# A square root moved one place forward in ScalarE's queue, and one PSUM evacuation split by K tile, at the start of a TensorE-bound kernel

## The chip, the cores and the metric

The kernel runs on one core of one Trainium2 chip. The metric is device microseconds of one launch. Engines are called as in the profile: PE is the matmul engine (PEld its weight loads), ACT is ScalarE, DVE is VectorE, POOL is GpSimd. All runs used here were of the fast state, with a mean granted PE clock of 0.999 or 1.0; where the text below calls a run slow, it means a longer run within that state. A run with several rounds was timed beside the kernel before on the same chip.

## The reference, cut to what matters

```python
xn = layernorm(x)                      # x: 2048 tokens x 512, bf16
y  = x + S5(xn) + SwiGLU(xn)           # S5: complex diagonal scan over the tokens
# SwiGLU: (silu(xn @ w_gate) * (xn @ w_up)) @ w_down, hidden size 1376
```

Only the start matters here: before the first gate matmul can run, tokens must be loaded, normalised and transposed. The kernel works in 4 chunks of 512 tokens. Chunk 0 is handled in 4 tiles of 128 tokens, each in halves of 256 columns (two K tiles of 128).

## The kernel before: the parts that matter

Every operation is added to a graph. A list scheduler orders ACT, DVE and POOL from estimated durations (`est`) and from order constraints (`od`, `order=`); PE keeps the order in which its tasks are added. Each engine then runs its list strictly in order. Statistics of chunk 0 (cuts marked with `# ...`):

```python
def ln_stat0(a, order):
    # DVE: bn_aggr -> mv[a] ...
    hold["sd%d" % a] = g.add("act", ... func=AF.Sqrt ...)      # the square root, on ACT
# DVE's order: r reciprocal, n normalise a half, b statistics of a half, s aggregate + square root
last = ln_stat0(0, (bn_full(0),))
for op, a, h in (("r", 0, 0), ("n", 0, 0), ("b", 1, 0), ("b", 1, 1), ("s", 1, 0), ("n", 0, 1), ("b", 2, 0),
                 ("r", 1, 0), ("n", 1, 0), ("n", 1, 1), ("b", 2, 1), ("s", 2, 0), ("b", 3, 0),
                 ("r", 2, 0), ("n", 2, 0), ("n", 2, 1), ("b", 3, 1), ("s", 3, 0), # ...
```

Transposes, evacuations and gate matmuls. One PSUM bank holds the transposes of every half tile:

```python
def xt_tile_fine(a, h):
    # PE: two 128x128 transposes of xn half h of tile a into PSUM bank `slot`
    # tiles 0 to 2: ACT copies 128x256 from PSUM to xnT ("xTev", hold["ev<a><h>"]); tile 3: DVE does
# ...
for q in range(4):                                   # token tile q
    for k0, k1 in ((0, 2), (2, 3), (3, 4)) if q == 0 else ((0, 2), (2, 4)):
        for n, (i, bk) in enumerate(tiles):          # 7 column blocks of the gate
            if k0 == 0 and n == (2 if q == 0 else 1): xt_tile_fine(q, 1)
            if k0 == 2 and n == 1 and q < 3:          xt_tile_fine(q + 1, 0)
            # PE: gate matmuls of K tiles k0 to k1-1, 128 columns each
seq = ["sd0", "ev00", "sd1", "ev01", "ev10", "ev11", "sd2", "ev20", "sd3", "ev21"]   # ACT's order
for a_, b_ in zip(seq, seq[1:]):
    hold[b_].od.add(hold[a_])
```

So tile 2's square root `sd2` stands behind `ev11`, the evacuation of tile 1's second half.

Of the kernel before, what the change touches and what calls it, by code (L numbers as in the profile page):

```python
# [14 lines left out]
AF = mybir.ActivationFunctionType  # L15
# [234 lines left out]
def bass_parallel_sum__ssm_conv_s5__swiglu_ffn__prompt_kernel(  # L250
# [30 lines left out]
    g = _Graph()  # L281
    es = ExitStack()
    with es:
        block = es.enter_context(nc.Block(no_gpsimd_drain=True))

        def sb(name, shape, dt):
            return es.enter_context(nc.sbuf_tensor(name, shape, dt))
# [11 lines left out]
        wg = sb("wg", [128, KT, FT * 128], B16)  # L299
# [30 lines left out]
        sd0 = sb("sd0", [128, 4], F32)  # L330
# [38 lines left out]
        def next_pair():  # L369
            for _ in range(NB // 2):  # L370
                b = 2 * (pair_ctr[0] % (NB // 2))
                pair_ctr[0] += 1
                if not (b in reserved or _bank_live(b) or _bank_live(b + 1)):
                    return b
            raise AssertionError("all PSUM pairs live")
# [4 lines left out]
        def BK(b):  # L380
            return [("bk", b, 0), ("bk", b, 1)]
# [60 lines left out]
        def loads_stage_b2():  # L442
# [13 lines left out]
              reads=[("ones",)], writes=[("ident",)], name="ident", est=300)  # L456
        g.add("pool", lambda e: e.iota(iot[:], pattern=[[1, TP]], base=0, channel_multiplier=0, allow_small_or_imprecise_dtypes=True),
              writes=[("iot",)], name="iota", est=1000)
# [3 lines left out]
        def act_table(func, order):  # L462
            g.add("act", lambda e: e.activation(out=sm[:, NSM - 1, 0:1], in_=epst[:], func=func, bias=epst[:, 0:1]), reads=[("epst",)], writes=[("sm", "_warm")],
                  name="act_warm", est=1500, order=order)
# [3 lines left out]
        def pe_warm(n, w=512, bk=None):  # L468
            if bk is None:
                bk = next_pair()  # L470

            def mm(e, bk=bk):
                for _ in range(n):
                    inst = e.matmul(pbank[:, bk, 0:w], lhsT=one.to_broadcast([128, 128]), rhs=one.to_broadcast([128, w]), start=True, stop=True)  # L474
                return inst
            g.add("pe", mm, writes=BK(bk), name="pe_warm", est=n * w * 0.84, ninst=n)
# [29 lines left out]
        hold = {}  # L506
# [18 lines left out]
        def ln_chunk0():  # L525
            def bn_full(a, order=()):
                return g.add("dve", lambda e: e.bn_stats(out=st0[:, a, 0, :], in_=x_sb[:, a, :]), reads=[("x", a)], writes=[("st0", a, 0)], name="bnst%d" % a, est=640, order=order)
            def recip(a, order):
                return g.add("dve", lambda e: e.reciprocal(out=rstd[:, a:a + 1], in_=sd0[:, a:a + 1]), reads=[("sd0", a)], writes=[("rstd", a)],  # L529
                             name="rstd%d" % a, est=140, order=order)  # L530
# [3 lines that stand above are left out]
                             ("r", 2, 0), ("n", 2, 0), ("n", 2, 1), ("b", 3, 1), ("s", 3, 0),  # L534
                             ("r", 3, 0), ("n", 3, 0), ("n", 3, 1)):
                if op == "r":
                    last = recip(a, (last,))
                elif op == "n":
                    last = ln_half(a, h, (last,))
                elif op == "b":  # L540
                    last = bn_half(a, h, (last,))
                else:
                    last = ln_stat0(a, (last,))
            hold["xn3"] = last
# [15 lines left out]
        def xt_tile_fine(a, h):  # L560
            slot = xt_pair[0]
            par = a == 3 and h == 1

            def tr2(e):
                if par:
                    e.transpose(out=ptr[:, slot, 512:524], in_=prow[:], identity=ident[0:12, 0:12])  # L566
                for j in range(2):
                    kt = h * 2 + j
                    inst = e.transpose(out=ptr[:, slot, j * 128:(j + 1) * 128],  # L569
                                       in_=xn_sb[:, a % NXN, kt * 128:(kt + 1) * 128], identity=ident[:])  # L570
                return inst
            g.add("pe", tr2, reads=[("xh", a, h), ("ident",)] + [("prow", k) for k in range(3) if par], writes=BK(slot), name="xT%d_%d" % (a, h), est=2 * 64 + 100 * par, ninst=2 + par)
            dst, src = xnT[:, 0, a % 4, 2 * h:2 * h + 2, :], ptr[:, slot, 0:256].rearrange("p (k t) -> p k t", k=2)
            wr = [("xnTh", a, h)] + ([("xnT", 0, a % 4)] if h else [])
            if a == 3:
                t = g.add("dve", lambda e: e.tensor_copy(out=dst, in_=src), reads=BK(slot), writes=wr, name="xTev%d_%d" % (a, h), est=320, order=(hold["xn3"],))
                if par:
                    g.add("dve", lambda e: e.tensor_copy(out=praw[:].rearrange("p k a -> p (k a)"), in_=ptr[:, slot, 512:524]),
                          reads=BK(slot), writes=[("praw", k) for k in range(3)], name="parTev", est=80, order=(t,))
            else:  # L580
                t = g.add("act", lambda e: e.activation(out=dst, in_=src, func=AF.Identity), reads=BK(slot), writes=wr, name="xTev%d_%d" % (a, h), est=340)  # L581
            hold["ev%d%d" % (a, h)] = t
# [154 lines left out]
        def ffn_mm(c, i, which, bk):  # L737
            fs = fsz[i]
            w = wg if which == "g" else wu

            def mm(e, bk=bk, w=w, i=i, fs=fs, c=c):
                for kt in range(KT):
                    inst = e.matmul(pbank[0:fs, bk, :].rearrange("p (j t) -> p j t", j=4), lhsT=w[:, kt, i * 128:i * 128 + fs], rhs=xnT[:, c % 2, :, kt, :],  # L743
                                    start=(kt == 0), stop=(kt == KT - 1))
                return inst
            g.add("pe", mm, reads=wres("wg" if which == "g" else "wu", i) + [("xnT", c % 2, j) for j in range(4)],
                  writes=BK(bk), name="mm_%s%d_%d" % (which, c, i), est=4 * 216, ninst=4)
# [17 lines left out]
        def ffn_gate_quarters(pairs):  # L765
            banks = {ip: next_pair() for ip in pairs}
            reserved.update(banks.values())
            tiles = [(2 * ip + k, banks[ip] + k) for ip in pairs for k in range(2)]
            xt_pair[0] = tiles.pop()[1]
            wbank = tiles[-1][1]  # L770
            pe_warm(9, 512, wbank)
            pe_warm(2, 128, wbank)
            ln_chunk0()
            xt_tile_fine(0, 0)
            pe_warm(2, 256, wbank)
            for q in range(4):
                for k0, k1 in ((0, 2), (2, 3), (3, 4)) if q == 0 else ((0, 2), (2, 4)):
                    for n, (i, bk) in enumerate(tiles):
                        if k0 == 0 and n == (2 if q == 0 else 1):
                            xt_tile_fine(q, 1)  # L780
                        if k0 == 2 and n == 1 and q < 3:
                            xt_tile_fine(q + 1, 0)
                        def mm(e, bk=bk, i=i, q=q, k0=k0, k1=k1):
                            for kt in range(k0, k1):
                                inst = e.matmul(pbank[:, bk, q * 128:(q + 1) * 128], lhsT=wg[:, kt, i * 128:(i + 1) * 128], rhs=xnT[:, 0, q, kt, :],  # L785
                                                start=(kt == 0), stop=(kt == KT - 1))
                            return inst
                        g.add("pe", mm, reads=[("wg", "a%d" % max(k - 1, 0)) for k in range(k0, k1)] + [("xnTh", q, k0 // 2)], writes=BK(bk), name="mm_gq%d_%d_%d" % (i, q, k0),
                              est=(k1 - k0) * 56, ninst=k1 - k0)
            reserved.clear()  # L790
            seq = ["sd0", "ev00", "sd1", "ev01", "ev10", "ev11", "sd2", "ev20", "sd3", "ev21"]
            for a_, b_ in zip(seq, seq[1:]):
                hold[b_].od.add(hold[a_])
            act_table(AF.Silu, (hold["ev21"],))
            hold["evac"] = g.tasks[-1]
            ffn_mm(0, NQ, "g", xt_pair[0])
            for ip in pairs:
                silu_pair(0, ip, banks[ip])
# [273 lines left out]
```

## Time and profile before

| | before |
|---|---|
| time, median of 3 runs | 180.33 us (180.17 to 180.47) |
| span of the profiled run | 178.5 us |
| PE between 30 and 170 us | busy 140.0 of 140.0 us |
| PE weight loads idle before tile 2's transposes | 0.63 us |

First the busy line and the chain line of the profile page of the kernel before.

```profile
PE 174.5 (98%) x936; PEld 83.8 (47%) x936; DVE 163.1 (91%) x285; ACT 87.5 (49%) x110; POOL 11.3 (6%) x21
...
PE 97%; ACT 1%; DVE 0%; issue 0%
```

Then a row of the table by windows (window and length in us, busy us and instruction count of PE, PEld, DVE, ACT, POOL, then clock and DMA):

```profile
30.00:170.00 140.00, 140.00 (x678) 64.10 (x676) 137.69 (x195) 65.35 (x76) 6.32 (x4) 1.00 0.15 40
```

From tile 2's transposes at 9.45 us to its last matmul, which ends at 176.15 us, PE never pauses in this trace. A microsecond saved on another engine in that stretch is worth nothing; one that lets PE start its long run sooner should be worth a microsecond. ACT between 7 and 9 us, in the timeline of the kernel before (start, duration, what; in brackets the idle time before it and who ended it; L581 is an evacuation, L521 a square root):

```profile
7.29 0.38 ACT L581 ACTIVATE xnT<-pb 128x256 bf16<-128x256 bf16 x1 [0.43 <-PE pb L569]
8.24 0.38 ACT L581 ACTIVATE xnT<-pb 128x256 bf16<-128x256 bf16 x1 [0.57 <-PE pb L569]
8.52 0.29 ACT L521 ACTIVATE sd<-mv,epst 128x1 f32<-128x1 f32 x1
```

DVE around that root, same view (L519 is the aggregate of tile 2's statistics, L529 the reciprocal of the root; tile 2 is normalised from 9.04 us on):

```profile
7.50 0.21 DVE L519 BATCH_NORM_AGGREGATE mv<-st 128x2 f32<-128x12 f32 x1
...
8.84 0.17 DVE L529 RECIPROCAL rstd<-sd 128x1 f32<-128x1 f32 x1 [0.84 <-ACT sd L521]
```

and PE's weight loads, same view (L569 are transposes, L785 gate matmuls, L743 the first full-width matmuls):

```profile
5.86 0.24 PEld L785 LDWEIGHTS pb<-xnT,wg 128*128 128x128 bf16 x4 [0.60 <-issue]
6.15 0.11 PEld L569 LDWEIGHTS pb<-ident,xn_sb 128*128 128x128 bf16 x2
...
7.99 0.82 PEld L785 LDWEIGHTS pb<-xnT,wg 128*128 128x128 bf16 x14
9.44 0.12 PEld L569 LDWEIGHTS pb<-ident,xn_sb 128*128 128x128 bf16 x2 [0.63 <-DVE xn_sb L514]
...
13.86 0.15 PEld L743 LDWEIGHTS pb<-xnT,wg 128*128 128x128 bf16 x2
```

The reader is to see the idle 0.57 us in front of ACT's evacuation at 8.24, the square root behind it, and 0.63 us in which PE waits for what depends on that root. Evacuation and root were queued in the wrong order: the root's input was ready at 7.71 us (end of DVE's aggregate), while ACT stood idle.

### The profile page before, as it was taken

Reading aid. Unit: us, or ns where it says so; the run is one execution under the profiler, and the core shown is the slowest. Engines: PE = TensorE matmul, PEld = TensorE weight load, DVE = VectorE, ACT = ScalarE, POOL = GpSimd, SP = SyncE. Lnnn points to the kernel's source line nnn. Section 1 sums busy time; section 2 is a strip of 40 time slices with the busy share of each in tenths; the row PEclk is TensorE's granted clock in tenths of the full one; section 3 lists DMA queues with packets and bytes.
Section 4 is the critical chain, followed back from the end, with each engine's and each line's share of the span. In section 5 each row is a group of like instructions: output and inputs, shape, how many; then the busy total and the mean of one; then the engine's idle time right before and its main releaser. Section 6 shows DMA issues by size and latency. Waiting matters only on the chain.

```text
span 178.5 us, 2422 instructions
## 1 busy us (share of the span) xinstructions
PE 174.5 (98%) x936; PEld 83.8 (47%) x936; DVE 163.1 (91%) x285; ACT 87.5 (49%) x110; POOL 11.3 (6%) x21
## 2 busy tenths in 40 slices
PE   8989999999999999999999999999999999999994
PEld 2785444444444444444444444444444444444743
DVE  2768988997999999999999999999899999999933
ACT  4459999799999765024565651000965620000000
POOL 3014200130000000260000000000000000000000
PEclk9999999999999999999999999999999999999999
DMA  5995563569450000001510000001000000001022
GB/s 169 376 326 118 119 121 119 128 133 333 131 94 0 0 0 0 0 29 62 123 26 0 0 0 4 0 29 59 29 0 4 0 0 0 0 0 49 14 88 88
DMA packets 22978, 12.37 MB, mean 69 GB/s; under 512 B 15192, under 2 KB 22968, under 8 KB 22968
## 3 DMA queue, kind: packets, MB, share of 16 engines
q1 hardware_dynamic: 22472, 11.54, 23.6%
q10 hardware_dynamic: 496, 0.69, 1.1%
q8 instruction: 7, 0.11, 0.3%
q14 instruction: 3, 0.02, 0.0%
HBM read 6.46 MB, written 2.10 MB: 48 GB/s over the span
## 4 chain that ended last, share of the span: by engine, by line
PE 97%; ACT 1%; DVE 0%; issue 0%
PE pb L743 35%; PE pb L940 21%; PE pb L953 16%; PE pb L857 15%; PE pb L785 3%; PE pb L474 2%; PE pb L820 2%; PE pb L830 1%; PE pb L569 1%; ACT xnT L581 0%; DVE xn_sb L514 0%; DVE x_sb L958 0%; ACT sd L521 0%; DVE rstd L529 0%; PE pb L566 0%
## 5 line engine op out<-in xcount | busy, mean ns | idle before, releaser
L897 DVE TENSOR_TENSOR_SCAN rot<-sm,car,rot 128x512 bf16<-128x512 f32 x32 | 39.0, 1267 | 0.1
L940 PE MATMUL pb<-wd,hT 128*128 128x512 bf16 (+3 forms) x198 | 38.8, 356 | 0.0
L743 PE MATMUL pb<-xnT,wu 128*128 128x512 bf16 x160 | 37.3, 379 | 0.0
L743 PE MATMUL pb<-xnT,wg 128*128 128x512 bf16 x132 | 31.3, 380 | 0.0
L953 PE MATMUL pb<-W,hss 128*128 128x512 bf16 (+2 forms) x144 | 28.3, 356 | 0.0
L857 PE MATMUL pb<-xnT,BT 128*128 128x512 bf16 x128 | 28.1, 379 | 0.0
L940 PEld LDWEIGHTS pb<-wd,hT 128*128 128x128 bf16 (+1 forms) x198 | 18.5, 97 | 19.9
L755 ACT ACTIVATE sg<-pb 128x1024 bf16<-128x1024 f32 x20 | 20.1, 1024 | 9.2 <-PE pb L743 8.1
L743 PEld LDWEIGHTS pb<-xnT,wu 128*128 128x128 bf16 x160 | 15.6, 98 | 18.9 <-issue 0.2
L810 ACT ACTIVATE uf<-pb 128x1024 bf16<-128x1024 f32 x20 | 20.5, 1027 | 7.2 <-PE pb L743 6.1
L953 PEld LDWEIGHTS pb<-W,hss 128*128 128x128 bf16 x144 | 13.4, 98 | 14.3
L743 PEld LDWEIGHTS pb<-xnT,wg 128*128 128x128 bf16 x132 | 12.7, 98 | 15.7 <-issue 0.4
L857 PEld LDWEIGHTS pb<-xnT,BT 128*128 128x128 bf16 x128 | 12.5, 98 | 15.1
L864 ACT ACTIVATE u_sb<-pb 128x1024 bf16<-128x1024 f32 x16 | 16.2, 1021 | 5.9 <-PE pb L857 5.5
L958 DVE TENSOR_TENSOR x_sb<-pb,x_sb 128x512 bf16<-128x512 f32 (+2 forms) x18 | 11.1, 623 | 3.5 <-PE pb L953 3.5
L812 DVE TENSOR_TENSOR hT<-sg,uf 128x1024 bf16<-128x1024 bf16 x20 | 13.5, 684 | 0.6 <-ACT uf L810 0.5
L503 ACT ACTIVATE xn_sb<-x_sb,nmr,rstd 128x512 bf16<-128x512 bf16 x8 | 6.0, 803 | 9.7 <-DVE nmr L500 9.7
L839 ACT ACTIVATE sg<-pb 96x1024 bf16<-96x1024 f32 x2 | 2.0, 1020 | 17.1 <-PE pb L820 17.1
L888 DVE TENSOR_TENSOR rot<-u_sb,cosT 128x2048 bf16<-128x2048 bf16 x8 | 9.8, 1221 | 0.4 <-ACT u_sb L864 0.4
L888 DVE TENSOR_TENSOR rot<-rot,cosT 128x2048 bf16<-128x2048 bf16 x8 | 9.7, 1217 | 0.1
L888 DVE TENSOR_TENSOR rot<-u_sb,sin 128x2048 bf16<-128x2048 bf16 x8 | 9.8, 1220 | 0.0
L888 DVE TENSOR_TENSOR rot<-rot,sin 128x2048 bf16<-128x2048 bf16 x8 | 9.7, 1217 | 0.0
(78 smaller groups left out, 143.1 us busy)
## 6 DMA issues: line engine op xcount, KB each, us to landing
out_dram<-x_sb SPq DMA_DIRECT2D x15, 128.0 KB, 1.7
x_sb<-in_A_x_dram SPq DMA_DIRECT2D x3, 512.0 KB, 7.3
wd<-in_B_w_down_dram SPq DMA_DIRECT2D x1, 1280.0 KB, 6.8
wu<-in_B_w_up_dram SPq DMA_DIRECT2D x1, 768.0 KB, 5.0
wu<-in_B_w_up_dram SPq DMA_DIRECT2D x1, 608.0 KB, 7.2
x_sb<-in_A_x_dram SPq DMA_DIRECT2D x4, 128.0 KB, 3.4
wg<-in_B_w_gate_dram SPq DMA_DIRECT2D x1, 480.0 KB, 6.0
wg<-in_B_w_gate_dram ACTq DMA_DIRECT2D x1, 448.0 KB, 3.7
```

Of the source, the lines that this page charges most:

```text
L503: g.add("act", lambda e, a=a: e.activation(out=xn_sb[:, a % NXN, :], in_=x_sb[:, a, :], func=AF.Identity, scale=rstd[:, a:a + 1], bias=nmr ...
L743: inst = e.matmul(pbank[0:fs, bk, :].rearrange("p (j t) -> p j t", j=4), lhsT=w[:, kt, i * 128:i * 128 + fs], rhs=xnT[:, c % 2, :, kt, :], ...
L755: g.add("act", lambda e: e.activation(out=sg[rows, sl, 0:n, :].rearrange("p a t -> p (a t)"), in_=pair_f32(rows, bk, 512 * n), func=AF.Sil ...
L810: g.add("act", lambda e: e.activation(out=uf[rows, ul, 0:n, :].rearrange("p a t -> p (a t)"), in_=pair_f32(rows, bk, 512 * n), func=AF.Ide ...
L812: g.add("dve", lambda e: e.tensor_tensor(out=hT[rows, hb, i0:i0 + n, :], in0=sg[rows, sl, 0:n, :], in1=uf[rows, ul, 0:n, :], op=ALU.mult), ...
L857: inst = e.matmul(pbank[:, bk, :].rearrange("p (j t) -> p j t", j=4), lhsT=BT[:, ri, kt, pt * 128:(pt + 1) * 128], rhs=xnT[:, c % 2, :, kt ...
L864: g.add("act", lambda e: e.activation(out=u_sb[:, us].rearrange("p r t -> p (r t)"), in_=pair_f32(slice(0, 128), b0), func=AF.Identity), r ...
L888: tt = lambda out, a, b, op, r, w, nm: g.add("dve", lambda e: e.tensor_tensor(out=out, in0=a, in1=b, op=op), reads=r, writes=w, name="%s_% ...
L897: g.add("dve", lambda e, A0=A0, A1=A1, k=k, ri=ri, pt=pt: e.tensor_tensor_scan(out=A1[:, k, ri, :], data0=rr[:, pt:pt + 1].to_broadcast([1 ...
L940: inst = e.matmul(pbank[:, bk, 0:nc_], lhsT=hT[0:fs, hb, i, lt * 128:(lt + 1) * 128], rhs=wd[0:fs, i, c0:c0 + nc_], start=(i == 0), stop=F ...
L953: inst = e.matmul(pbank[:, bk, 0:nc_], lhsT=hss[:, hb, pt, ri, lt * 128:(lt + 1) * 128], rhs=W12[:, ri, pt, c0:c0 + nc_], start=False, sto ...
L958: g.add("dve", lambda e, bk=bk, a=a, c0=c0, nc_=nc_: e.tensor_tensor(out=x_sb[:, a, c0:c0 + nc_], in0=pbank[:, bk, 0:nc_], in1=x_sb[:, a, ...
```

## The change

The intent: (A) let tile 2's square root use ACT's idle time ahead of tile 1's second evacuation; (B) split tile 0's first evacuation, and the gate matmuls that read it, by K tile, so that the first matmul waits for 128 columns instead of 256. (The gate matmuls' `reads` follow the split.)

```diff
+            elif a == 0 and h == 0:
+                for j in range(2):
+                    t = g.add("act", lambda e, j=j: e.activation(out=dst[:, j], in_=src[:, j], func=AF.Identity), reads=BK(slot), writes=[("xnTq", j)], # ... est=240
+                    # the first is hold["ev0a"], the second hold["ev00"]
@@
-                for k0, k1 in ((0, 2), (2, 3), (3, 4)) if q == 0 else ((0, 2), (2, 4)):
+                for k0, k1 in ((0, 1), (1, 2), (2, 3), (3, 4)) if q == 0 else ((0, 2), (2, 4)):
@@
-                        if k0 == 0 and n == (2 if q == 0 else 1):
+                        if k0 == 0 and n == (4 if q == 0 else 1):
@@
-            seq = ["sd0", "ev00", "sd1", "ev01", "ev10", "ev11", "sd2", "ev20", "sd3", "ev21"]
+            seq = ["sd0", "ev0a", "ev00", "sd1", "ev01", "ev10", "sd2", "ev11", "ev20", "sd3", "ev21"]
```

Four gate matmuls stand ahead of tile 0's second transposes in both versions: two column blocks times two K tiles before, four blocks times one K tile after.

More of the change, by code (lines that the diff above doesn't have):

```diff
@@ L579, in xt_tile_fine @@
                           reads=BK(slot), writes=[("praw", k) for k in range(3)], name="parTev", est=80, order=(t,))
+            elif a == 0 and h == 0:
+                for j in range(2):
+                    t = g.add("act", lambda e, j=j: e.activation(out=dst[:, j], in_=src[:, j], func=AF.Identity), reads=BK(slot), writes=[("xnTq", j)],
+                              name="xTev0_0%d" % j, est=240, order=(t,) if j else ())
+                    if j == 0:
+                        hold["ev0a"] = t
             else:
@@ L787, in mm @@
                             return inst
-                        g.add("pe", mm, reads=[("wg", "a%d" % max(k - 1, 0)) for k in range(k0, k1)] + [("xnTh", q, k0 // 2)], writes=BK(bk), name="mm_gq%d_%d_%d" % (i, q, k0),
+                        g.add("pe", mm, reads=[("wg", "a%d" % max(k - 1, 0)) for k in range(k0, k1)] + ([("xnTq", k0)] if q == 0 and k0 < 2 else [("xnTh", q, k0 // 2)]), writes=BK(bk), name="mm_gq%d_%d_%d" % (i, q, k0),
                               est=(k1 - k0) * 56, ninst=k1 - k0)
             reserved.clear()
-            seq = ["sd0", "ev00", "sd1", "ev01", "ev10", "ev11", "sd2", "ev20", "sd3", "ev21"]
+            seq = ["sd0", "ev0a", "ev00", "sd1", "ev01", "ev10", "sd2", "ev11", "ev20", "sd3", "ev21"]
             for a_, b_ in zip(seq, seq[1:]):
```

## The prediction

> **What bounds the kernel.** TensorE. In the chain of waits PE has 97% of the span. The table by windows has PE busy 140.0 of 140.0 us between 30 and 170 us, at granted clock 1.00. Hence a gain can only come from the start: PE has idle time there that nothing later hides. Time before is 180.33 us (span 178.5).
>
> **Where PE stands still early (timeline, weight-load row, 5 to 14 us).**
> 1. 9.44 us: tile 2's first transposes wait for DVE's normalised tile. The weight load before them ends its turn at 8.77 us (8.714 plus the regular 0.056 step), so about 0.67 us is lost. The chain lists the cause: ACT evacuation 8.24 to 8.63, square root 8.52 to 8.81, reciprocal 8.84, normalise 9.04 to 9.39, transposes 9.44.
> 2. Tile 0: the first gate matmul at 5.86 waits for the evacuation (5.36 to 5.75); the next transposes at 6.15 wait for DVE's second half of tile 0 (ends 6.10), 0.09 us lost; K tile 2 at 6.91 waits for the second evacuation (6.48 to 6.86), 0.13 us lost.
>
> **Part A, square root moved.** Nothing is added. Tile 2's statistics are ready at 7.71, when ACT has finished tile 1's first evacuation (7.67) and stays idle 0.57 us until the transposes for the second (8.24). So the square root (0.29 us) fits into idle time, 7.75 to 8.04, without delaying the evacuation. Reciprocal 8.07, normalise 8.27 to 8.62, transposes possible at 8.67, before PE gets there (8.77). The wait vanishes: 0.67 us, less about 0.04 us because the restart after a wait issues two loads closer together (15 ns instead of 56): 0.63 us. Repeating the sums for tile 3 (square root about 9.5, transposes possible 10.4, PE there at 10.55) shows no new wait.
>
> **Part B, split by K tile.** It removes one 128x256 evacuation (0.383 us) and adds two 128x128. The Trainium skill, "ScalarE: Activation LUTs", section "What ACT_TABLE_LOAD costs", gives 186 ns + 0.833 ns per column for immediate scale and bias: 399 ns for 256 (trace: 383), so my estimate is 293 ns for 128. The first four matmuls then start about 0.1 us earlier. But the transposes after four matmuls still wait for DVE until 6.15, and ten matmuls again follow before K tile 2, which waits for the same evacuation. Gain: 0 (-0.05 to +0.05).
>
> **How much reaches the end.** Up to 13.8 us everything on PE moves 0.63 us earlier. Later releases that do not move have slack over 0.63 us: gate columns landed at 10.7 (needed 13.2), B's second transposed load at 22.2 (needed 24.5), chunk 1's transposed activations at 26.5 (31.4). DVE does not move (its chunk 1 statistics wait for a load landing at 13.74), and ACT loses the gain again around 23 us behind DVE's tables, but PSUM banks are freed 2 us or more ahead. At the end the last SSM result is written at 166.3, needed at 168.4. So nearly all of it arrives.
>
> **Prediction: 179.70 us, range 179.40 to 180.05.** Faster by over 2%: 0.01; within 2%: 0.98; slower: 0.01.
>
> **What shows it.** A: square root near 7.75, no weight-load wait near 9.4, tile 2's transposes near 8.8, first full-width matmul (13.86) near 13.2, PE still without idle from 30 to 170. B: two evacuations near 0.29 us, first gate matmul near 5.76, the transposes still at 6.15, K tile 2 still at 6.91. If B matters, 6.15 or 6.91 moves.
>
> **What would make it wrong.** The static scheduler orders ACT and DVE from estimates that the change edits, so later work may be ordered otherwise; a wait on DVE late in the kernel could eat the gain; tile 3's chain could wait anew.

## The result, and the profile after

| | before | after |
|---|---|---|
| time, median of 6 runs | 180.30 us (180.17 to 180.61) | 179.94 us (179.57 to 180.28) |
| span of the profiled run | 178.5 us | 177.8 us |
| first full-width matmul's weight load | 13.86 us | 13.20 us |
| from there to the end of the span | 164.64 us | 164.65 us |

The ratio is 0.9976, with a 95% interval from 0.9959 to 0.9994. Ratios in this document are the mean time of one kernel's fast runs over the mean of the other's of the same rounds, so they are not quite the ratio of the medians quoted beside them.

The two lines of the page, of the kernel after (line numbers below L581 in the file move by up to 6):

```profile
PE 173.7 (98%) x928; PEld 83.8 (47%) x936; DVE 163.2 (92%) x285; ACT 87.7 (49%) x111; POOL 9.2 (5%) x21
...
PE 95%; DMA 1%; DVE 1%; issue 0%; ACT 0%
```

Its row of the table by windows:

```profile
30.00:170.00 140.00, 139.63 (x671) 64.17 (x676) 137.03 (x195) 64.65 (x74) 3.96 (x4) 1.00 0.16 41
```

Weight loads are again 676 there; the missing 0.37 us of PE go with matmul records that this trace lacks. ACT in the timeline of the kernel after (L582 is the split evacuation, L587 the others, L521 the roots):

```profile
5.26 0.45 ACT L582 ACTIVATE xnT<-pb 128x128 bf16<-128x128 bf16 x2 [0.96 <-PE pb L569]
...
7.26 0.38 ACT L587 ACTIVATE xnT<-pb 128x256 bf16<-128x256 bf16 x1 [0.50 <-PE pb L569]
7.75 0.29 ACT L521 ACTIVATE sd<-mv,epst 128x1 f32<-128x1 f32 x1
8.21 0.38 ACT L587 ACTIVATE xnT<-pb 128x256 bf16<-128x256 bf16 x1 [0.17 <-PE pb L569]
```

DVE, same kernel and view (tile 2 is now normalised from 8.27 us on):

```profile
7.50 0.21 DVE L519 BATCH_NORM_AGGREGATE mv<-st 128x2 f32<-128x12 f32 x1
...
8.07 0.16 DVE L529 RECIPROCAL rstd<-sd 128x1 f32<-128x1 f32 x1
```

and PE's weight loads (L749 are now the first full-width matmuls):

```profile
5.65 0.24 PEld L791 LDWEIGHTS pb<-xnT,wg 128*128 128x128 bf16 x4 [0.49 <-issue]
6.05 0.11 PEld L569 LDWEIGHTS pb<-ident,xn_sb 128*128 128x128 bf16 x2 [0.16 <-DVE xn_sb L514]
...
7.96 0.82 PEld L791 LDWEIGHTS pb<-xnT,wg 128*128 128x128 bf16 x14
8.74 0.15 PEld L569 LDWEIGHTS pb<-ident,xn_sb 128*128 128x128 bf16 x2
...
13.20 0.59 PEld L749 LDWEIGHTS pb<-xnT,wg 128*128 128x128 bf16 x4
```

The root runs at 7.75, inside the idle time; the evacuation starts at 8.21 us (8.24 before); tile 2's transposes follow at 8.74 without a wait. The split evacuations run, and the gate matmuls start a little sooner (0.72 us after tile 0's transposes at 4.93, instead of 0.82 after those at 5.04), but the weight loads then stand idle 0.16 us for DVE where they stood idle 0.05 us. What the split gives, the next wait takes: from tile 0's first transposes to its second ones it is 1.11 us before and 1.12 us after, and to K tile 2 it is 1.88 us in both.

Two things did not fit the prediction smoothly. The median of the six runs moved 0.36 us and not 0.63. And the six runs spread over 0.7 us. (The kernel before spreads as much: its 37 runs lie between 180.17 and 180.97 us. So a spread of this size is not peculiar to the changed kernel.) The profiles themselves moved 0.66 us at the first full-width matmul, of which 0.10 us is a start that came early (tile 0's load landed at 3.03 instead of 3.14 us), and nothing was lost behind it: 164.64 and 164.65 us. So the experiments had two questions: which part earns the gain, and what makes the runs of one kernel differ.

### The profile page after: what moved, and what is told of

Same layout as the page of the kernel before. It is cut to its first block, busy times and chain, and to the rows that moved or that the text cites. A ratio compares the mean times of both kernels' runs of the same rounds, so it can differ in the third digit from the quotient of the medians.

```text
span 177.8 us, 2417 instructions
## 1 busy us (share of the span) xinstructions
PE 173.7 (98%) x928; PEld 83.8 (47%) x936; DVE 163.2 (92%) x285; ACT 87.7 (49%) x111; POOL 9.2 (5%) x21
## 4 chain that ended last, share of the span: by engine, by line
PE 95%; DMA 1%; DVE 1%; issue 0%; ACT 0%
PE pb L749 36%; PE pb L946 21%; PE pb L863 16%; PE pb L959 15%; PE pb L791 4%; PE pb L826 2%; DMA x_sb<-in_A_x_dram 1%; PE pb L836 1%; PE pb L569 1%; DVE st L527 0%; DVE xn_sb L514 0%; ACT sd L521 0%; DVE x_sb L964 0%; ACT xnT L582 0%; DVE mv L519 0%
## 5 line engine op out<-in xcount | busy, mean ns | idle before, releaser
L946 PE MATMUL pb<-wd,hT 128*128 128x512 bf16 (+3 forms) x194 | 38.1, 355 | 0.2
L749 PE MATMUL pb<-xnT,wu 128*128 128x512 bf16 x160 | 37.3, 379 | 0.0
L749 PE MATMUL pb<-xnT,wg 128*128 128x512 bf16 x132 | 31.3, 379 | 0.0
L749 PEld LDWEIGHTS pb<-xnT,wu 128*128 128x128 bf16 x160 | 15.6, 98 | 18.9 <-issue 0.2
L749 PEld LDWEIGHTS pb<-xnT,wg 128*128 128x128 bf16 x132 | 12.7, 98 | 15.7 <-issue 0.8
```

What stands on the lines that cost most here:

```text
L749: inst = e.matmul(pbank[0:fs, bk, :].rearrange("p (j t) -> p j t", j=4), lhsT=w[:, kt, i * 128:i * 128 + fs], rhs=xnT[:, c % 2, :, kt, :], ...
L946: inst = e.matmul(pbank[:, bk, 0:nc_], lhsT=hT[0:fs, hb, i, lt * 128:(lt + 1) * 128], rhs=wd[0:fs, i, c0:c0 + nc_], start=(i == 0), stop=F ...
```

## The experiments

Eleven runs were made, of nine different kernels (the changed one among them); all results were correct. All times in us; "before" is the kernel before.

| run | median (range), runs | before, median | ratio (95% interval) |
|---|---|---|---|
| e1: the changed kernel again | 179.71 (179.60 to 180.43), 5 | 180.36 | 0.9961 (0.9946 to 0.9975) |
| e2: root exchanged by hand only | 179.66 (179.55 to 179.82), 5 | 180.36 | 0.9959 (0.9946 to 0.9972) |
| e3: split only | 180.22 (180.17 to 180.51), 5 | 180.36 | 0.9992 (0.9979 to 1.0005) |
| e4: root too early | 180.17 (180.08 to 180.92), 6 | 180.36 | 0.9992 (0.9976 to 1.0008) |
| e5: statistics later | 179.63 (179.59 to 179.91), 5 | 180.27 | 0.9965 (0.9953 to 0.9977) |
| e6: tile 2's load late | 180.39 (180.22 to 181.08), 6 | 180.27 | 1.0010 (0.9994 to 1.0025) |
| e7: both | 179.80 (179.63 to 180.28), 6 | 180.27 | 0.9972 (0.9959 to 0.9985) |
| e8: short warm-up | 181.44 (180.69 to 182.02), 6 | 180.27 | 1.0056 (1.0032 to 1.0081) |
| e9: the changed kernel, third time | 179.65 (179.55 to 180.08), 5 | 180.34 | 0.9961 (0.9949 to 0.9973) |
| e10: as e5, beside e9 | 179.66 (179.62 to 179.71), 5 | 180.34 | 0.9958 (0.9944 to 0.9971) |
| e11: as e5 without the split | 179.71 (179.59 to 179.98), 5 | 180.34 | 0.9962 (0.9949 to 0.9974) |

### e1 (and e9): the changed kernel again

No edit.

> The changed kernel as it is, timed again, because six runs left the gain at 0.24% with an interval from 0.06% to 0.41%. My theory (the square root's move removes a 0.63 us wait and nothing is given back later) expects a gain of 0.55 to 0.70 us, ratio near 0.9965. The rival (half of the gain is given back or only reached in some runs) expects about 0.35 us, ratio near 0.998. In the trace, my theory expects the time from the first full-width matmul to the end to be the same as before, 164.6 us.

> The changed kernel once more, as the partner of the two below on the same chip. Expected: median 179.6 to 179.9, and one or two of its runs at 180.1 to 180.5 (runs in which tile 2's load lands late).

The ratio is 0.9961 both times, a gain of 0.7 us by the means and 0.65 and 0.69 us by the medians. From the first full-width matmul to the end it took 164.64 us both times. So nothing is given back later, and the first result, 179.94, was low on gain because three of its six runs were slow ones (180.06, 180.19, 180.28). e1's profile happened to fall on a slow run (180.43 us) and shows why it was slow; that is the start of e5. e9's profile is of a usual run, and its weight loads (tile 0's first transposes and the first full-width matmuls) make a cleaner pair with the kernel before than the first profile:

```profile
5.07 0.11 PEld L569 LDWEIGHTS pb<-ident,xn_sb 128*128 128x128 bf16 x2 [0.61 <-DVE xn_sb L514]
...
13.26 0.59 PEld L749 LDWEIGHTS pb<-xnT,wg 128*128 128x128 bf16 x4
```

Counted from tile 0's first transposes (5.04 us before, 5.07 here), tile 2's transposes, at 8.80 us, come 0.67 us earlier than before (3.74 instead of 4.41 us) and the first full-width matmul 0.63 us earlier (8.20 instead of 8.83 us).

### e2: the exchange by hand

On the kernel before, after the static order is made:

```diff
         streams = _schedule(g.tasks, engs)
+        act = streams["act"]
+        names = [t.name for t in act]
+        sd2 = act.pop(names.index("sd2"))
+        act.insert([t.name for t in act].index("xTev1_1"), sd2)
```

> The kernel before with two ACT instructions exchanged by hand after the static order is made: tile 2's square root in front of tile 1's second evacuation. No split, and the order of everything later stays that of before. My theory expects the whole gain of the changed kernel (0.55 to 0.70 us; equal to the repeat of the changed kernel within 0.1 us), with no wait of PE for tile 2's transposes. Rival 1 (the split by K tile brings part of it) expects a smaller gain than the changed kernel's. Rival 2 (the gain comes from the later ACT and DVE work that the static scheduler put in another order) expects none.

The change had also made the scheduler reorder small parameter work on DVE and the sine tables on ACT between 12 and 34 us. Here all of that stays as before; ACT's two instructions are the only difference. The whole gain is there (0.9959 against e1's 0.9961). The timeline of weight loads of this run:

```profile
7.98 0.82 PEld L785 LDWEIGHTS pb<-xnT,wg 128*128 128x128 bf16 x14
8.76 0.15 PEld L569 LDWEIGHTS pb<-ident,xn_sb 128*128 128x128 bf16 x2
```

No wait is left in front of tile 2's transposes. Rivals 1 (the split) and 2 (the later order) both fall.

### e3: the split alone

The changed kernel with the root put back:

```diff
-            seq = [..., "ev10", "sd2", "ev11", "ev20", "sd3", "ev21"]
+            seq = [..., "ev10", "ev11", "sd2", "ev20", "sd3", "ev21"]
```

> The changed kernel with the square root put back behind tile 1's second evacuation: the split alone. My theory expects the time of before within 0.1 us: the first gate matmul about 0.1 us earlier after its transposes, but the second transposes still at about 6.15 us behind DVE's half tile, and K tile 2 still behind the second evacuation. Rival 1 expects a gain of 0.1 to 0.3 us.

0.9992, interval including 1: at most 0.2% and most likely nothing. The profile is finer: from tile 0's first transposes to the first full-width matmul it takes 8.83 us, as in the kernel before. Its weight loads show the reason and the old wait together:

```profile
5.69 0.24 PEld L791 LDWEIGHTS pb<-xnT,wg 128*128 128x128 bf16 x4 [0.49 <-DMA wg<-in_B_w_gate_dram]
6.09 0.11 PEld L569 LDWEIGHTS pb<-ident,xn_sb 128*128 128x128 bf16 x2 [0.16 <-DVE xn_sb L514]
...
9.38 0.11 PEld L569 LDWEIGHTS pb<-ident,xn_sb 128*128 128x128 bf16 x2 [0.63 <-DVE xn_sb L514]
```

The load that the first line names had landed at 5.20 us; what came last was the evacuation, which ends at 5.58 us.

### e4: the root too early

The hand exchange of e2 with `"xTev1_0"` in place of `"xTev1_1"`: the root goes ahead of tile 1's first evacuation.

> The kernel before with tile 2's square root moved one place further, in front of tile 1's FIRST evacuation. My theory says the place matters because ACT takes its queue in order: the evacuation that could start at 7.29 us must wait for statistics that are ready at 7.71 and for the root's 0.29 us, so it ends near 8.4 instead of 7.67 and PE waits some 0.6 us for it: no gain against before (within 0.15 us), though the root itself runs as early as in the good version. A rival by which only the root's own start counts expects the full gain of 0.6 us.

0.9992: the gain is gone, although the root starts as early as in the good version. ACT's timeline:

```profile
7.67 0.29 ACT L521 ACTIVATE sd<-mv,epst 128x1 f32<-128x1 f32 x1 [0.84 <-DVE mv L519]
7.88 0.36 ACT L581 ACTIVATE xnT<-pb 128x256 bf16<-128x256 bf16 x1
8.73 0.38 ACT L581 ACTIVATE xnT<-pb 128x256 bf16<-128x256 bf16 x1 [0.49 <-PE pb L569]
```

The root waits 0.84 us for its statistics, and the evacuation, whose data were ready at about 7.3, waits behind it until 7.88. Tile 1's second transposes slip from 7.87 (e2) to 8.36 us. The Trainium skill, "TensorE: Matmul & The Clock Gate", section "Architectural detail", says that ACT and DVE take their queues strictly first in, first out; this run agrees. The move is worth something after the evacuation that can already run and before the one that can't; one place further forward it brought nothing that can be told from zero.

### e5: statistics of tile 2 later

e1's slow profile, DVE's timeline (L509 statistics of a half tile, L529 reciprocal, L514 normalise):

```profile
6.84 0.43 DVE L509 BATCH_NORM_STATS2 st<-x_sb 128x6 f32<-128x256 bf16 x1 [0.77 <-DMA x_sb<-in_A_x_dram]
7.19 0.15 DVE L529 RECIPROCAL rstd<-sd 128x1 f32<-128x1 f32 x1
7.37 0.60 DVE L514 TENSOR_SCALAR xn_sb<-x_sb,mv,rstd 128x256 bf16<-128x256 bf16 x2
```

DVE waits 0.77 us for tile 2's load, and tile 1's reciprocal and normalise, which don't need that load, wait behind it. In the trace's landing events that load completed at 6.82 us here; in the profiles of before and after, at 5.86 and 5.98. In this same profile, though, the PE clock rose late too (at 6.67 us: the matmuls start 0.107 us apart until then and 0.056 us apart after it). So there were two theories: A, the late load makes the slow runs; B, the late rise of the clock does. The edit of the changed kernel:

```diff
-("s", 1, 0), ("n", 0, 1), ("b", 2, 0), ("r", 1, 0), ("n", 1, 0), ("n", 1, 1), ("b", 2, 1), ("s", 2, 0), ("b", 3, 0),
+("s", 1, 0), ("n", 0, 1), ("r", 1, 0), ("n", 1, 0), ("b", 2, 0), ("b", 2, 1), ("s", 2, 0), ("n", 1, 1), ("b", 3, 0),
```

> The changed kernel with DVE's queue in another order at the start: tile 2's first half statistics, which must wait for tile 2's load, go behind tile 1's reciprocal and first half of the normalise (and tile 1's second half behind tile 2's statistics). In the profile of the repeat (180.43 us) that load landed at 6.82 instead of 5.9 to 6.0, DVE stood 0.77 us in front of it, and tile 1's normalise waited behind. Theory A (the load's landing makes the slow runs) expects no run over 180.0 us, a median of 179.5 to 179.7, and tile 1's transposes near 6.9 even when the load is late. Theory B (the late rise of the PE clock makes the slow runs; it rose at 6.67 in that profile, at 4.09 and 5.07 in two others) expects the same spread as the changed kernel, runs up to 180.4 among them.

No run was over 179.91 us, as theory A said. But five runs prove little; e6 and e7 test the cause directly.

### e6 and e7: the load late on purpose

e6 is the changed kernel with this edit, e7 is e5 with it:

```diff
-        x_load(2)
         act_q.append(wg_load("a1", 2, 3, eng="act", order=(act_q[-1],)))
         wg_load("a2", 3, 4)
+        x_load(2)
```

> The changed kernel with tile 2's load issued behind the last block of gate weights instead of ahead of it, so that it lands some 0.6 us later in every run. Theory A expects all runs slow, median 180.1 to 180.4. Theory B expects the time of the changed kernel, 179.7, with the same spread.

> Both edits together: tile 2's load late, and DVE's order without the wait for it in tile 1's chain. Theory A expects at most 0.2 us over the run with the new order alone, so 0.3 us or more less than with the late load alone. Theory B expects no difference between this and the run with the late load alone.

The load landed at 6.81 (e6) and 6.67 us (e7). DVE in e6:

```profile
6.83 0.43 DVE L509 BATCH_NORM_STATS2 st<-x_sb 128x6 f32<-128x256 bf16 x1 [0.78 <-DMA x_sb<-in_A_x_dram]
7.17 0.15 DVE L529 RECIPROCAL rstd<-sd 128x1 f32<-128x1 f32 x1
```

and in e7:

```profile
6.22 0.17 DVE L529 RECIPROCAL rstd<-sd 128x1 f32<-128x1 f32 x1 [0.15 <-ACT sd L521]
6.42 0.34 DVE L514 TENSOR_SCALAR xn_sb<-x_sb,mv,rstd 128x256 bf16<-128x256 bf16 x1
6.69 0.75 DVE L509 BATCH_NORM_STATS2 st<-x_sb 128x6 f32<-128x256 bf16 x2
```

All six runs of e6 were slow (median 180.39; the move's gain is wiped out), and the new order takes back 0.6 us of it by the medians (179.80). The intervals of the two ratios don't overlap. Tile 1's transposes stood at 7.76 in e6, at 6.98 in e7. So a late landing of this one load alone makes a slow run of the changed kernel. In e6's profile the gate matmuls start 0.056 us apart from the first one on, so its clock was not late. e7 still has runs of 180.01 and 180.28; they weren't profiled, and their cause is open.

### e8: a short warm-up

The changed kernel with `pe_warm(4, 512, wbank)` in place of `pe_warm(9, 512, wbank)`.

> The changed kernel with 4 instead of 9 wide warm-up matmuls, so that PE stands idle before the first transposes and the clock rises later: measures what a late rise costs by itself. Theory B expects a large loss: up to 28 gate matmuls of 128 columns per token tile at about 0.107 us instead of 0.056, that is up to 1.4 us per tile in which the clock stays low. Theory A alone says nothing here; a loss below 0.3 us would show that the clock matters little in this stretch.

1.0056 against before: about 1.7 us slower than the changed kernel, which had 0.9961. It was run at another time. The clock rose at 10.15 us. PE in its timeline:

```profile
0.83 2.08 PE L474 MATMUL pb<-const-bfloat16-1.0 128*128 128x512 bf16 x6 [0.83 <-PEq L1063]
5.03 0.39 PE L569 MATMUL pb<-ident,xn_sb 128*128 128x128 bf16 x2 [2.12 <-DVE xn_sb L514]
...
7.86 1.81 PE L791 MATMUL pb<-xnT,wg 128*128 128x128 bf16 x15
```

15 matmuls took 1.81 us; the same 15 took 1.00 us in the profile of before. So a late rise is costly once it reaches into the gate matmuls. With nine warm-up matmuls the rise lay between 4.08 and 6.67 us in the eight profiles that record it, while the first gate matmul's weight load starts at 5.65 to 5.89. In the one at 6.67 (e1) it held K tile 2 back to 7.14, against 6.91 in the profile before; that was then hidden by the longer wait for DVE. In e11's profile nothing hides it: the clock isn't recorded there, but matmuls start 0.107 us apart until 6.26 us, K tile 2 comes 2.10 us after tile 0's first transposes (1.88 in e9), and the first full-width matmul 8.42 us after them (8.20 in e9). Theory B thus isn't refuted: a late rise can add about 0.2 us to a run. It isn't what made e6 slow: that profile has an early rise.

### e10 and e11: is there a version that beats both?

e10 is e5 again, beside e9. e11 is e2 with e5's order of statistics and no split.

> The changed kernel with tile 2's statistics behind tile 1's normalise, again, beside the changed kernel. Theory A (a late load makes the slow runs) expects the same fastest runs, 179.5 to 179.6, and a mean 0.1 to 0.2 us lower, for lack of runs above 180.0.

> The kernel before with the two ACT instructions exchanged by hand and the same new order of statistics, without the split. If the split is worth nothing here too, it equals the run with the split within 0.1 us. If the split was useless only because other waits covered it, this one is slower by about 0.1 us.

e10's range is narrow (179.62 to 179.71), though in its profile the load landed at 6.28 us, late. But its median is e9's, and the ratios 0.9958 and 0.9961 can't be told apart: the means differ by 0.06 us, not by the 0.1 to 0.2 expected. Over all, 5 of 16 runs of the changed kernel were above 180.0 us, and 0 of 10 with the new order: suggestive, and few enough to be chance (e2, with the old order, had none in 5 either). The mechanism is shown by e6 against e7; that ordinary runs gain from it in the mean is not. e11 equals e10 within their intervals (expected within 0.1 us: 179.71 against 179.66), so the split is worth nothing here either.

## Why the prediction was right

The prediction of 179.70 us held: 179.94 at first, then 179.71 and 179.65 in the repeats, all inside the range, and the class "within 2%" was right.

- **The bound.** PE bound the kernel and had idle time only at the start. Shown: in all profiles of these kernels, fast or slow, the time from the first full-width matmul to the end is 164.64 to 164.65 us. Everything that a profiled run gained or lost lies before that matmul.
- **Part A, 0.63 us.** Root near 7.75: 7.75. Transposes near 8.8: 8.74. First full-width matmul near 13.2: 13.20. Alone (e2) it brings 0.41% by the means, 0.74 us, with an interval of 0.51 to 0.97 us that holds the predicted 0.63. In the pair of profiles: 0.66 us moved, minus 0.10 for the earlier landing of the first load, plus 0.07 us that the kernel after lost again waiting for tile 2's load before tile 1's transposes, is 0.63. That 13.20 itself came out is partly luck, since these two offsets nearly cancel; e9's pair needs no such correction and shows the prediction's own sum, a wait of 0.67 us gone and 0.63 us of it left at the first full-width matmul.
- **Part B, 0.** The two evacuations took 0.277 and 0.272 us where the estimate from the skill's page was 0.293. Counted from tile 0's first transposes, the first gate matmul came 0.1 us sooner, and the next transposes and K tile 2 did not, as said (by the clock of the profile they stood at 6.05 and 6.81 instead of 6.15 and 6.91, because the whole start was 0.10 us early); alone (e3) it brings 0.08%, not told from zero. A shorter wait in front of a second wait that doesn't move was worth nothing.
- **How much reaches the end.** All of it. The prediction feared the static scheduler's new order. The order did change (DVE's parameter work, ACT's sine tables), and it cost and brought nothing: e2, without it, has the same time within the intervals.
- **What the prediction missed.** It took the arrival of loads as fixed. Tile 2's load stood only just ahead of its use (landed 5.86, used 6.01 us), and in DVE's queue tile 1's work stands behind it. That doesn't change the typical gain, but it can make a run 0.8 us slower, as e1's profile and e6 show. Of 16 runs of the changed kernel, 5 were 0.4 to 0.8 us above the usual 179.65; three of these were among the first six, so the medians first showed 0.36 us of a gain of 0.65. Only one of the five was profiled; that the others had the same cause is likely, not shown. The late rise of the clock, which the prediction also left out, is a second, smaller source (about 0.2 us in e11's profile).

## What to carry to other kernels

When an engine runs its queue in order, look for a short instruction queued behind a long wait although its own input is ready: moving it into that idle time cost nothing here, and the right place is found from ready times (after what can already run, before what can't yet), not from "as early as possible". Before splitting a step to start the next one sooner, look for the second wait directly behind it. And when one kernel's runs spread more than its gain, profile a slow run: here it showed a load that landed late, waited for ahead of work in the same queue that did not need it.

## What the Trainium skill lacked or had wrong

- "ScalarE: Activation LUTs", section "What ACT_TABLE_LOAD costs": the formula of 186 ns + 0.833 ns per column gives 293 ns for 128 and 399 ns for 256 columns; these evacuations from PSUM took 0.277 and 0.272 us, and 0.383 us, so 16 to 21 ns less. The slope fits.
- "TensorE: Matmul & The Clock Gate", section "Part 1: The HAM clock gate", has the rise about 4 us into sustained activity, give or take 0.5 us from run to run. In eight profiles with the same nine wide warm-up matmuls, begun at 0.83 us, it came at 4.08 to 6.67 us, so 3.2 to 5.8 us after the first matmul. With four, it came at 10.15 us, and cost about 1.7 us of 180 (0.9%), close to the 1% that the page gives as the most to expect.
- "DMA: Bandwidth & Descriptors", section "Latency and other measured facts", gives 0.2 us on average and 2 us at high load for an HBM access, but I found no page that says how far the landing of one and the same load moves from run to run. Tile 2's 128 KB, issued at the same place in every one of these kernels, landed between 5.53 and 6.82 us over eleven profiles, which is enough to decide between a fast and a slow run.
